# First-layer blocks of 512 columns as halves of 256, a changed order of each chunk's first blocks, and shorter zero matmuls

## The chip, the cores and the metric

The kernel runs on one core of one Trainium2 chip, in one launch. The metric is the device time of an execution in microseconds (us), the median over runs. Three runs of the kernel before took 183.96 to 184.36 us, median 184.15.

The core has a matrix engine (TensorE, PE in the profile; PEld are its weight loads), a vector engine (VectorE, DVE), an engine for functions of single elements (ScalarE, ACT), a general one (GpSimd, POOL), and a sequencer that mostly issues transfers (SyncE, SP). 16 DMA engines move data. TensorE writes into PSUM, an accumulator memory; the others read it from there. Engines run their own instruction streams and wait for each other through semaphores.

## What is computed

A recurrent linear attention over 768 time steps (batch 4, 8 heads, head size 48), and then a two-layer network with a SiLU over the 3072 resulting rows of 384 values:

```python
for t in range(S):
    kt, vt, rt = (k[:, :, t], v[:, :, t], r[:, :, t])
    cur = np.einsum('bhd,bhe->bhde', u[None] * kt, vt)
    y[:, :, t] = np.einsum('bhd,bhde->bhe', rt, state + cur)
    state = w[None, :, :, None] * state + np.einsum('bhd,bhe->bhde', kt, vt)
x = y.transpose(0, 2, 1, 3).reshape(B * S, H * D)
h = x @ w_in                                # 384 -> 2048
out = (h * (1.0 / (1.0 + np.exp(-h)))) @ w_out   # 2048 -> 384
```

All inputs and the output are float32; the kernel does most matmuls in 16 bits.

## The kernel before

*Chunks and units.* Time is cut into six chunks of 128 steps. A unit is one chunk of one batch element, so there are 24 units, numbered chunk by chunk: units 0 to 3 are chunk 0, and so on. Within a unit the recurrence is made parallel: r and k are scaled by powers of w, the part inside the chunk (for later units inside each half of it) is a masked product of r and k, and the part of earlier steps comes through a carried state.

*The attention part of an iteration.* The main loop (L748) takes units in pairs, i and i + 1, so that a chunk has two iterations: `b` is 0 for units 0 and 1 of the chunk, and 2 for units 2 and 3. On TensorE an iteration is: `sums` (L478: products of k and v, 32 matmuls of 48 columns with both halves, 16 in the last chunk), `product_halves` (L455: r times k, 32 products in float32, seen in the trace as 64 matmuls), some fillers (below), `outputs_halves` (L552 and L561, 32 matmuls each: the carried state's part and the part inside the chunk), and `turn` (L272: transposes of the next pair's r, and of k where that isn't done by transfers). VectorE masks the product (L462), forms the state (L495, L509) and adds a bonus term to the outputs (L401, `evict_halves`). `turn_y_dma` (L584) then has a DMA transpose write y into the tile `xT` of the chunk, 4 units x 3 parts x 128 columns, which the first layer reads. Later units' k goes through another DMA transpose (L321).

*The network part.* The first layer is cut into 16 blocks of 128 of the 2048 inner values. `l1(sc, 0, B, f)` for chunk `sc` and block `f` does three matmuls (L606, one for each 128 of the 384 inputs) over all four units of the chunk at once, 512 columns, into a PSUM tile `hps`, then ACT's SiLU (L615) into `gT`. In chunks 0 and 1 some blocks are done for two units at a time: 256 columns, two blocks to a PSUM tile. The second layer, `l2` (L628), is done unit by unit: four parts of four matmuls with 384 columns, then a copy (L634) and a store (L638). The very last unit's is split (L653).

*Fillers.* These pieces are put into a list and taken from it at fixed places of the loop by `fill(n)`: after `product_halves`, after the turn, and later in the iteration, so that TensorE has work while other engines prepare the next step of the attention. A chunk gives 16 fillers of the first layer (`first(sc)` for chunks 2 to 5) and 16 of the second (`second(sc)`). They are appended at L790, after the second pair's `turn_y_dma`; what is still in the list from the chunk before goes first. A filler of the first layer is one block. After the loop `fill` empties the list (L822).

*The beginning.* For units 0 to 5 the order of all work is written out by hand in the string `order` (L717); a word like `2*spin` calls `spin(2)`. `spin` (L178) multiplies zeros (the tile `idle`) into a PSUM tile that nobody reads; the order has six such matmuls right after `clear` near the start, and nine more, in groups of one or two, between the real work up to unit 7. `lk8`, `lr8` and the like are loads of a unit's k or r into one of eight buffers, issued on SP.

*PSUM.* `hps`, `ops`, `sp`, `yp`, `yT`, `zs` and `bc` share four buffers (tag "moe"), given out in turn; a new tile waits for the readers of the one that had its buffer. The product and the turn use two tiles of their own (`att`).

The whole order is fixed at build time (`manual_schedule`), so each engine runs its instructions exactly as written.

Of the kernel before, what the change touches and what calls it, by code (L numbers as in the profile page):

```python
# [8 lines left out]
FP = mybir.dt.float32  # L9
# [7 lines left out]
def kernel(  # L17
# [11 lines left out]
    nc = tc.nc  # L29

    B, H, S, D = r.shape
    C = 128
# [6 lines left out]
    NFT = DFF // 128  # L39
    NQ = HD // 128  # L40
# [7 lines left out]
    ps = ctx.enter_context(tc.tile_pool(name="ps", bufs=1, space=bass.MemoryType.PSUM))  # L48
    ctx.enter_context(tc.manual_schedule())

    def unit(i):
        return divmod(i, B)
# [15 lines left out]
    win = [big.tile([128, NQ, 512], F16, name=f"win{g}") for g in range(4)]  # L68
# [36 lines left out]
    idle = cst.tile([128, 512], F16)  # L105
# [69 lines left out]
            nc.scalar.copy(out=dst[i][:, :, D:64],  # L175
                           in_=idle[:, 0:128].rearrange("p (h d) -> p h d", h=H))

    def spin(n):  # L178
        zs = ps.tile([128, 512], FP, name="zs", tag="moe", bufs=4)
        for _ in range(n):  # L180
            nc.tensor.matmul(zs, idle[:, 0:128], idle, start=True, stop=True)

    def clear():
        for t in att:
# [18 lines left out]
    def spread_row(name, src):  # L203
        spread[name] = ps.tile([128, HD], FP, name="bc", tag="moe", bufs=4)
        nc.tensor.matmul(spread[name], ones, src, start=True, stop=True)
# [369 lines left out]
    xts = {}  # L575
# [23 lines left out]
    hpss = {}  # L599

    def l1_mm(sc, b0, nb, ft):
        m = B // nb
        hps = hpss[b0, ft] = ps.tile([128, m, nb * C], FP, name="hps", tag="moe", bufs=4)
        for f in range(m):
            for q in range(NQ):
                nc.tensor.matmul(hps[:, f, :].rearrange("p (b t) -> p b t", b=nb), win[(ft + f) // 4].rearrange("p q (t c) -> p q t c", c=4)  # L606
                                 [:, q, :, (ft + f) % 4],
                                 xts[sc][:, b0:b0 + nb, q, :],
                                 start=(q == 0), stop=(q == NQ - 1))

    def l1_silu(sc, b0, nb, ft):
        if sc not in gts:
            gts[sc] = wrk.tile([128, NFT, B * C], F16, name="gT", bufs=2)
        m = B // nb
        nc.scalar.activation(out=gts[sc][:, ft:ft + m, b0 * C:(b0 + nb) * C], in_=hpss[b0, ft],  # L615
                             func=AF.Silu)

    def l1(sc, b0, nb, ft):
        l1_mm(sc, b0, nb, ft)
        l1_silu(sc, b0, nb, ft)  # L620
# [56 lines left out]
        return [lambda ft=ft: l1(sc, 2, 2, ft) for ft in range(0, NFT, 2)]  # L677

    def first(sc):
        return [lambda f=f: l1(sc, 0, B, f) for f in range(NFT)]  # L680

# [2 lines left out]
    halved = [lambda ft=ft: l1(1, 0, 2, ft) for ft in range(0, NFT, 2)]  # L686

    def piece(word, f):
        b0, ft = word.split(".")
        f(0, *blocks[b0], int(ft))  # L690
# [6 lines left out]
        "wy": lambda: columns(nc.scalar, wpT, w, 0), "lnw": powers_r, "eK": exponents_k,  # L697
        "lamK": powers_k, "uc": copy_u, "wb": lambda: spread_row("w", w_row),
        "ub": lambda: spread_row("u", u_row), "lnwb": ln_w, "lamC": powers_c, "lamH": powers_h, "lamN": powers_n,
        "tab": silu_table, "clear": clear, "spin": lambda: None, "H": lambda: halved.pop(0)(),  # L700
    }
    unit_steps = {
        "T": turn, "rT": lambda i: decay_one(i, 0), "kT": lambda i: decay_one(i, 1),
# [12 lines left out]
    }  # L716
    order = """  # L717
        ur kz0 id itr lr0 wy pd0 ak0 cz2 kz3 itc wr mk wx cz1 mh lnw eK cg3 lamK kz4 kz1 lk1
        id16 lr1 pd3 lr3 lk3 clear 6*spin lv0 cg0 lv1 kz7 lr2 ak2 ku0 lv3 lr5 kz2 lv2 ub pd1 lv4
        lr4 lk4 lv5 pd2 lk5 lk7 lr6 lk6 uc T0 1*spin T1 lr7 lv7 kT0 pa4 rT0 ru0 ku1  # L720
        v160 pd5 lv6 rT1 kz6 rd0 kT1 wb ru1 P0 n0 2*spin rd1 P1 vu0 lnwb T2 n1 v161 2*spin
        pd7 lamC lamH lamN pa6 i_q0 V0 v162 tab rT2 e0 kT2 ku2 T3 1*spin yT0 V1 kz5 vu1 i_q1 ru2
# [9 lines left out]
    for word in order.split():  # L732
        if "*" in word:
            n, word = word.split("*")
            spin(int(n))
        if word in steps:
            steps[word]()
        elif word[0] == "L":
            piece(word[1:], l1_mm)
        elif word[0] == "G":  # L740
            piece(word[1:], l1_silu)
        else:
            unit_steps[word[:-1]](int(word[-1]))
# [4 lines left out]
    for i in range(B + 2, NU, 2):  # L748
        sc, b = unit(i)
# [39 lines left out]
        if b:  # L789
            fillers.extend((first(sc) if sc > 1 else rest_first(sc)) + second(sc))  # L790
# [62 lines left out]
```

## Time and profile before

| | us |
|---|---|
| median of three runs | 184.15 |
| the profiled execution | 185.49 |
| its span, first to last instruction | 183.8 |
| busy: TensorE matmuls | 174.5 |
| busy: TensorE weight loads (overlap the matmuls) | 113.9 |
| busy: GpSimd | 129.3 |
| busy: VectorE | 117.0 |
| busy: ScalarE | 115.8 |

One execution was recorded by the hardware profiler. A group row names the line, the engine, the operation, what is written from what, its form and count, and then the busy time, the mean duration in ns, and the idle time of the engine just before with what ended it. A row of the chain of waits has the start, the length and the piece of work, followed back from the last instruction; "issue" is time for which the profile knows no cause. A row of the timeline has start, length, engine, line, operation and count, where equal neighbours are merged. A row of the windows has a stretch, its length, TensorE's busy time and instruction count in it, the granted clock, the mean busy share of the DMA engines, and GB/s. The length of a merged row reaches to the end of its last instruction, and a matmul's end overlaps the next one's start: the duration of a matmul of 512 columns is 380 ns in the mean, while the next starts 216 ns after it. The TensorE clock was granted in full over the whole span.

### The profile page before, as it was taken

What the parts mean: (1) busy time and instruction counts of PE and PEld (TensorE: products, weight loads), DVE (VectorE), ACT (ScalarE), POOL (GpSimd) and SP (SyncE); (2) the same over time, 40 slices, a digit from 0 to 9 for tenths busy, and PEclk for the clock granted to TensorE, in tenths of its full rate; (3) what the DMA queues carried; (4) which work ended last, traced back from release to release, by engine and by line L of the source; (5) the groups of instructions that cost most, each with busy time, mean ns of one, the idle gap of its engine ahead of it and who ended that gap; (6) DMA issues with size and microseconds to landing.
All of it is one profiled execution on the core that took longest, in us unless ns stands there. A gap on an engine that the chain in (4) does not pass through costs nothing.

```text
span 183.8 us, 6611 instructions
## 1 busy us (share of the span) xinstructions
PE 174.5 (95%) x2801; PEld 113.9 (62%) x2801; DVE 117.0 (64%) x231; ACT 115.8 (63%) x208; POOL 129.3 (70%) x179
## 2 busy tenths in 40 slices
PE   7977899999899999999899999999999999999993
PEld 2555786588666976656556555657656566555562
DVE  5999728897977985865775955776944974000120
ACT  4471787699145797398597488797588781299200
POOL 7999999898899979869979769879769700000000
PEclk9999999999999999999999999999999999999999
DMA  5999999899697799999599999499799201410022
GB/s 95 238 192 216 178 175 200 154 224 225 129 189 210 114 202 184 199 183 202 114 178 177 162 209 213 92 183 160 183 197 250 49 4 46 128 43 0 10 79 86
DMA packets 102865, 27.89 MB, mean 152 GB/s; under 512 B 97586, under 2 KB 102324, under 8 KB 102836
## 3 DMA queue, kind: packets, MB, share of 16 engines
q1 hardware_dynamic: 98224, 23.86, 66.5%
q0 software_dynamic: 2176, 3.15, 10.1%
q10 hardware_dynamic: 2436, 0.46, 1.3%
q8 instruction: 22, 0.36, 0.8%
q14 instruction: 7, 0.06, 0.1%
HBM read 20.45 MB, written 4.72 MB: 137 GB/s over the span
## 4 chain that ended last, share of the span: by engine, by line
PE 72%; POOL 17%; DMA 5%; issue 5%; ACT 0%; POOLq 0%
PE ops L628 33%; PE hps L606 26%; DMA kin<-in_k_dram 5%; PE att L455 4%; POOL ku L240 4%; POOL rku_f L245 3%; PE att L272 3%; POOL vu L258 2%; POOL kc L248 2%; PE yp L552 2%; PE sp L478 2%; PE ops L653 1%; PE yp L561 1%; POOL win L84 1%; POOL wout L89 1%
## 5 line engine op out<-in xcount | busy, mean ns | idle before, releaser
L606 PE MATMUL hps<-xT,win 128*128 128x512 f16 (+1 forms) x360 | 66.3, 338 | 0.1
L615 ACT ACTIVATE gT<-hps 128x512 f16<-128x512 f32 x96 | 55.3, 597 | 12.2 <-PE hps L606 8.9
L628 PE MATMUL ops<-wout,gT 128*128 128x384 f16 x368 | 62.9, 326 | 0.1
L606 PEld LDWEIGHTS <-win 128*128 128x128 f16 x360 | 39.0, 114 | 21.1 <-issue 0.4
L628 PEld LDWEIGHTS <-gT 128*128 128x128 f16 x368 | 35.0, 98 | 23.9 <-ACT gT L615 0.8
L401 DVE TENSOR_TENSOR y<-yp,vu 64x384 f16<-64x384 f32 (+1 forms) x34 | 18.9, 555 | 11.3 <-PE yp L561 5.5
L245 POOL TENSOR_TENSOR rku_f<-ku,u_bc 128x384 f32<-128x384 f32 x24 | 24.2, 1010 | 1.4
L240 POOL TENSOR_TENSOR ku<-kin,rin 128x384 f32<-128x384 f32 x24 | 24.2, 1007 | 0.7 <-DMA rin<-in_r_dram 0.6
L258 POOL TENSOR_TENSOR vu<-vin,rku 128x384 f32<-128x384 f32 x24 | 19.6, 828 | 6.8 <-DVE rku L253 6.8
L289 DVE TENSOR_TENSOR rT<-att,lamR 112x512 f16<-112x512 f32 (+1 forms) x26 | 17.8, 684 | 4.2 <-PE att L272 3.8
L326 ACT COPY kT<-blocks 112x1024 uint16<-112x1024 uint16 x14 | 15.6, 1160 | 7.6 <-DMA blocks<-planes 7.5
L634 ACT COPY osb<-ops 128x384 f32<-128x384 f32 x20 | 9.4, 475 | 16.5 <-PE ops L628 12.5
L495 DVE TENSOR_TENSOR s<-sp,sdec 112x384 f32<-112x384 f32 x10 | 5.6, 557 | 16.0 <-PE sp L478 15.4
L636 DVE COPY osb<-ops 128x384 f32<-128x384 f32 x3 | 1.7, 557 | 21.3 <-PE ops L628 21.3
L462 DVE TENSOR_TENSOR am<-att,maskH 128x1024 f16<-128x1024 f32 x10 | 12.2, 1224 | 3.5 <-PE att L455 3.5
L343 DVE TENSOR_TENSOR rX<-att,lamR 48x256 f16<-48x256 f32 x32 | 13.5, 421 | 0.5
L263 ACT CAST v<-vin 128x384 f16<-128x384 f32 x16 | 7.9, 510 | 8.4 <-DMA vin<-in_v_dram 8.3
L253 DVE TENSOR_REDUCE rku<-rku_f 128x8 f32<-128x384 f32 x24 | 12.4, 542 | 0.9 <-POOL rku_f L245 0.9
L314 POOL TENSOR_TENSOR lnw_bc<-kin,lamN 128x384 f32<-128x384 f32 x7 | 7.0, 1001 | 8.0 <-DMA kin<-in_k_dram 6.4
L434 ACT CAST s1h<-s 48x384 f16<-48x384 f32 x16 | 8.2, 510 | 6.7 <-DVE s L495 6.6
L455 PE MATMUL att<-rT,kT 48*64 48x64 f32 x640 | 11.9, 220 | 0.2 <-issue 0.2
L455 PEld LDWEIGHTS att<-rT,kT 48*64 48x64 f32 x640 | 10.6, 135 | 0.3 <-issue 0.3
(106 smaller groups left out, 214.0 us busy)
## 6 DMA issues: line engine op xcount, KB each, us to landing
rin<-in_r_dram SPq DMA_DIRECT2D x24, 192.0 KB, 4.0
vin<-in_v_dram SPq DMA_DIRECT2D x24, 192.0 KB, 4.6
out_dram<-osb SPq DMA_DIRECT2D x23, 192.0 KB, 3.2
kin<-in_k_dram SPq DMA_DIRECT2D x22, 192.0 KB, 3.5
win<-in_moe_w_in_dram POOLq DMA_DIRECT2D x4, 384.0 KB, 6.3
wout<-in_moe_w_out_dram POOLq DMA_DIRECT2D x4, 384.0 KB, 6.6
kin<-in_k_dram ACTq DMA_DIRECT2D x2, 192.0 KB, 3.7
xT<-y SPq DMA_TRANSPOSE x9, 2.8
```

Of the source, the lines that this page charges most:

```text
L240: eng.tensor_tensor(out=L(i)["ku"], in0=kin[i % NIN][:, :, 0:D], in1=rin[i % NIN][:, :, 0:D], op=ALU.mult)
L245: eng.tensor_tensor(out=L(i)["rku_f"], in0=L(i)["ku"], in1=u_bc, op=ALU.mult)
L253: nc.vector.tensor_reduce(out=L(i)["rku"], in_=L(i)["rku_f"], axis=mybir.AxisListType.X, op=ALU.add)
L258: eng.tensor_tensor(out=L(i)["vu"], in0=vin[i % NIN], in1=L(i)["rku"].unsqueeze(2).broadcast_to([128, H, D]), op=ALU.mult)
L289: nc.vector.tensor_tensor(out=L(i)[key].rearrange("p g (y t) -> p y g t", y=2), in0=L(i)["t"][0:PR, :, x], in1=lam, op=ALU.mult)
L326: nc.scalar.copy(out=L(i)["kT"].rearrange("p g t -> p (g t)").bitcast(U16) .rearrange("p (n y) -> p n y", y=2), in_=turned[0:PR, i % 2].re ...
L343: nc.vector.tensor_tensor(out=rx[here], in0=L(i)["t"][there, x, 0], in1=(lamM if by_planes(i) else lamR)[there, :, 0:HC], op=ALU.mult)
L401: nc.vector.tensor_tensor(out=y16[a], in0=y[b, 0:HD], in1=vu[a], op=ALU.add)
L455: nc.tensor.matmul(a[o0:o0 + HC, j, e, p, :], kT[r0:r0 + D, p, HC * x:HC * x + HC], rT[r0:r0 + D, p, HC * x:HC * x + HC], start=True, stop ...
L606: nc.tensor.matmul(hps[:, f, :].rearrange("p (b t) -> p b t", b=nb), win[(ft + f) // 4].rearrange("p q (t c) -> p q t c", c=4) [:, q, :, ( ...
L615: nc.scalar.activation(out=gts[sc][:, ft:ft + m, b0 * C:(b0 + nb) * C], in_=hpss[b0, ft], func=AF.Silu)
L628: nc.tensor.matmul(opss[b], gts[sc][:, ft, b * C:(b + 1) * C], wout[:, ft, :], start=(ft == 0), stop=(ft == NFT - 1))
```

## The change

Three edits, all in what TensorE is given:

- `first(sc)` no longer makes a filler of one whole block. A new function `l1_half` does a block for two units, 256 columns: three matmuls into the left or right half of the block's PSUM tile, and the SiLU over all 512 columns after the right half. A filler is now two halves.
- The order of a chunk's first two fillers: the first does units 0 and 1 of blocks 0 and 1, the second does units 2 and 3 of both. Every later filler does both halves of one block. In chunk 2 the last six blocks stay whole.
- `spin` takes a number of columns, 100 by default, and does five matmuls for each that it did before; the six at the start keep 512 columns (the word `long`).

```diff
-    def spin(n):
+    def spin(n, cols=100):
         zs = ps.tile([128, 512], FP, name="zs", tag="moe", bufs=4)
-        for _ in range(n):
-            nc.tensor.matmul(zs, idle[:, 0:128], idle, start=True, stop=True)
+        for _ in range(n * (512 // cols)):
+            nc.tensor.matmul(zs[:, 0:cols], idle[:, 0:128], idle[:, 0:cols], start=True, stop=True)
...
+    def l1_half(sc, b0, ft):
+        if b0 == 0:
+            hpss[0, ft] = ps.tile([128, 1, B * C], FP, name="hps", tag="moe", bufs=4)
+        for q in range(NQ):
+            nc.tensor.matmul(hpss[0, ft][:, 0, b0 * C:(b0 + 2) * C].rearrange("p (b t) -> p b t", b=2),
+                             win[ft // 4].rearrange("p q (t c) -> p q t c", c=4)[:, q, :, ft % 4],
+                             xts[sc][:, b0:b0 + 2, q, :],
+                             start=(q == 0), stop=(q == NQ - 1))
+        if b0:
+            l1_silu(sc, 0, B, ft)
...
     def first(sc):
-        return [lambda f=f: l1(sc, 0, B, f) for f in range(NFT)]
+        whole = 6 if sc == 2 else 0
+        halves = [(b0, f) for b0 in (0, 2) for f in range(2)]
+        halves += [(b0, f) for f in range(2, NFT - whole) for b0 in (0, 2)]
+        return [lambda n=n: [l1_half(sc, *h) for h in halves[n:n + 2]]
+                for n in range(0, len(halves), 2)] + [
+                    lambda f=f: l1(sc, 0, B, f) for f in range(NFT - whole, NFT)]
...
-        id16 lr1 pd3 lr3 lk3 clear 6*spin lv0 cg0 lv1 kz7 lr2 ak2 ku0 lv3 lr5 kz2 lv2 ub pd1 lv4
+        id16 lr1 pd3 lr3 lk3 clear 6*long lv0 cg0 lv1 kz7 lr2 ak2 ku0 lv3 lr5 kz2 lv2 ub pd1 lv4
...
-            spin(int(n))
+            spin(int(n), *((512,) if word == "long" else ()))
```

In the built programs TensorE has 3011 matmuls instead of 2801, each with a weight load. The instructions of the other four engines, their transfers included, stand in the same order as before.

More of the change, by code (lines that the diff above doesn't have):

```diff
@@ L699 @@
         "ub": lambda: spread_row("u", u_row), "lnwb": ln_w, "lamC": powers_c, "lamH": powers_h, "lamN": powers_n,
-        "tab": silu_table, "clear": clear, "spin": lambda: None, "H": lambda: halved.pop(0)(),
+        "tab": silu_table, "clear": clear, "spin": lambda: None, "long": lambda: None, "H": lambda: halved.pop(0)(),
     }
```

## The prediction

> **What bounds the kernel now.** I read the busy shares first, then who TensorE (PE) waited for, then the chain of work that ended last, and last the trace around two odd gaps.
>
> ```profile
> span 183.8 us, 6611 instructions
> ...
> PE 174.5 (95%) x2801; PEld 113.9 (62%) x2801; DVE 117.0 (64%) x231; ACT 115.8 (63%) x208; POOL 129.3 (70%) x179
> ...
> q8 instruction: 22, 0.36, 0.8%
> ```
>
> PE is busy 95%, the others 62 to 70%. The third line is the queue that brings instructions: 22 packets. PE has 2801 matmuls and 2801 weight loads; 5602/22 is 255, so a packet is one block of 256 PE instructions (16.4 KB), fetched while the program runs.
>
> PE's waits from 20 us on:
>
> ```profile
> PE att L272 <- DMA kin<-in_k_dram: 1.0, 2, 0.6
> PE yp L561 <- issue: 0.5, 1, 0.5
> PE att L272 <- issue: 0.4, 1, 0.4
> ...
> PE att L455 <- issue: 0.2, 1, 0.2
> ```
>
> Three are put down to "issue": nothing the profile can name. The chain shows where:
>
> ```profile
> 38.46 9.68 DMA kin<-in_k_dram
> ...
> 48.19 0.44 PE att L272 x8
> ...
> 73.20 0.37 PE yp L552 x32
> ...
> 74.44 5.31 PE ops L628 x32
> ...
> 87.05 0.37 PE yp L552 x32
> 87.42 0.12 PE yp L561 x13
> 87.54 0.51 issue
> 88.05 0.34 PE yp L561 x19
> ...
> 88.98 4.66 PE hps L606 x21
> ...
> 100.50 0.37 PE yp L552 x32
> ...
> 101.51 0.43 issue
> 101.94 0.44 PE att L272 x9
> 102.38 5.31 PE ops L628 x32
> ...
> 180.83 0.27 ACT osb L660
> ```
>
> Until 48.19 the end is set by POOL and then by a load of k that lands at 48.14; PE stood idle for it. From 48.19 to 180.8 the chain is PE work piece after piece, broken only by the two "issue" gaps. So what is saved or added on PE behind 48.19 counts in full, and what changes ahead of it is first swallowed by the wait for k.
>
> The gaps cut a run of equal matmuls in two (13 and 19 of L561's 32; seven transposes of L272, then nine), so no operand was late. An undisturbed stretch from the first L552 to the end of the turn takes 74.44 - 73.20 = 1.24 us. The two with gaps take 88.98 - 87.05 = 1.93 and 102.38 - 100.50 = 1.88. So 0.69 + 0.64 = **1.33 us** are lost.
>
> Busy time from the start to chosen moments, for the count of matmuls behind "x":
>
> ```profile
> 0.00:83.13 83.13, 77.79 (x1369) 1.00 0.97 184
> 0.00:88.05 88.05, 82.20 (x1497) 1.00 0.98 183
> 0.00:97.58 97.58, 91.70 (x1625) 1.00 0.96 181
> 0.00:101.94 101.94, 95.63 (x1752) 1.00 0.97 180
> ```
>
> From one gap's end to the other's are 255 matmuls. With weight loads and the few instructions that only wait, the kernel's instruction order puts the first late ones at 3010 and 3522: exactly two blocks apart. The short gap in L455 (the 0.2 above) is at 962, eight blocks ahead of 3010. I conclude that **PE starves at block borders**. A border is crossed each 256 instructions, and most cost nothing. These were reached too fast: the block ahead was entered at 83.13 and 97.58 (128 and 127 matmuls earlier), 4.92 and 4.36 us before work resumed. The fetches, each seen as one packet in a tenth of a microsecond, began only at 85.8 and 98.5:
>
> ```profile
> q8 instruction: 1, 0.02, 54.9%
> ...
> q8 instruction: 1, 0.02, 121.8%
> ```
>
> Bursts of small matmuls (sums, product, outputs, turn) eat a block quickly; L606 and L628 eat it slowly. The sequencer also works ahead: the earliest fetch began when PE was 303 instructions short of its block. So I measure a border's lead from PE being 303 short to PE arriving. By positions and starts in the trace the gaps' leads are 5.1 and 4.7 us, stall included; every other border behind 48 us had 5.9 or more and lost nothing. The early one at 962 had 6.4, in a stretch where fetches start later.
>
> The Trainium skill ("Runtime: NRT & Kernel Launch", section "Instruction fetch mechanics") has the same 256-instruction blocks, but says that crossing a border is one queue bump, "mostly hidden". The rows disagree at these two borders.
>
> **The change part by part.** *Halves: price on PE.* A block of `first` is three matmuls of 512 columns and becomes six of 256. Split are ten blocks in chunk 2 and 16 each in chunks 3 to 5: 58 blocks, 174 matmuls more. Both widths run already, in dense stretches:
>
> ```profile
> 61.77 4.78 PE L606 MATMUL hps<-xT,win 128*128 128x256 f16 x42
> 66.38 0.81 PE L628 MATMUL ops<-wout,gT 128*128 128x384 f16 x4
> ...
> 62.01 4.31 PE L606 MATMUL hps<-xT,win 128*128 128x256 f16 x38
> ...
> 160.04 9.66 PE L606 MATMUL hps<-xT,win 128*128 128x512 f16 x44
> ...
> L606 PE MATMUL hps<-xT,win 128*128 128x512 f16 x216 | 49.2, 380 | 0.0
> L606 PE MATMUL hps<-xT,win 128*128 128x256 f16 x144 | 17.1, 273 | 0.1
> ```
>
> Less the last one's duration, (4.31 - 0.273)/37 = 109.1 ns and (9.66 - 0.380)/43 = 215.8 ns from start to start. Two halves take 2.4 ns more than a whole: 174 x 2.4 = **+0.42 us**, all on the path. Bounds: 0, and 0.65 (with the lead-in from 61.77 to 66.38, 4.61 us over 42 are 109.8 ns). The weight load doubles with the matmul and is in the 109 ns.
>
> *Halves: place on the instruction grid.* This is the large term. In the built order PE has 416 instructions more, so every border falls elsewhere. A chunk's two iterations become 1025 instructions, four blocks and one, so from chunk 3 on the borders return to nearly the same four places, until chunk 5 has shorter sums. Behind 48 us they lie in L628 and split L606 work, except five in outputs (the 7th, 1st, 6th and 16th of L552's 32, the 10th of L561's 32) and one in chunk 5's sums. Their leads, with the durations of before put in the new order, are 6.7 us and more: the shortest, chunk 5's L561, has ahead of it 0.3 us of halves, 2.0 of L628, 0.3 of sums, 1.0 of product, 2.7 of L628, 0.5 of outputs. Before, 5.9 was enough and 5.1 not. So both stalls go: **-1.33 us**. Bounds: 0 if they aren't tied to the grid, -1.33 if they are; I take the latter.
>
> *Units 0, 1 first.* The first `fill` item of a chunk needs only the transpose of the chunk's first two units; the second pair's is due one filler (6 x 109 = 0.65 us) later. Chunk 3 shows why this matters once the stall at 101.5 is gone:
>
> ```profile
> 103.00 1.22 SPq L584 DMA_TRANSPOSE xT<-y  x1
> ...
> DMA to landing us min/median/max: 2.7/2.8/4.0
> ...
> 107.53 1.67 PE L606 MATMUL hps<-xT,win 128*128 128x512 f16 x7
> ```
>
> This is the slowest of the nine; it lands at 107.0, 0.5 us ahead of its first reader. The stall sat behind the outputs that feed it, so without the stall PE arrives 0.64 earlier: 0.1 late with whole blocks, 0.5 in time with halves. I cost it at zero; without the halves' order it would be +0.1. In exchange, two accumulators stay open through one filler and ACT gets the first two SiLUs together, the first 0.3 us later. Both end within the same `fill`, no other tile is taken between them, and the order on DVE, ACT, POOL and SP, their DMAs included, is unchanged: zero.
>
> *Short zero matmuls.* Nine of 512 columns become 45 of 100. Their price is bounded by the nearest narrower row:
>
> ```profile
> 179.79 1.00 PE L653 MATMUL ops<-wout,gT 128*128 128x128 f16 x15
> ...
> L653 PE MATMUL ops<-wout,gT 128*128 128x128 f16 x16 | 1.1, 219 | 0.0
> ```
>
> (1.00 - 0.219)/14 = 55.8 ns for 128 columns, so 45 cost at most 2.51 us; by columns (100/512 of 215.8, 42 ns) 1.90. The nine cost 1.94 now. That is -0.04 to +0.57, and I take +0.05 since 100 is near 128. None of it reaches the end: all nine stand ahead of 48.19, where these waits follow:
>
> ```profile
> 17.14 0.33 PE L380 MATMUL att<-rT,kT 48*64 48x128 f32 x4 [1.02 <-DVE rT L289]
> ...
> 48.19 0.32 PE L272 MATMUL att<-ident,kin 64*112 64x64 f32 x4 [0.56 <-DMA kin<-in_k_dram]
> ```
>
> Three of the nine come behind 17.14: at most 15 x 55.8 - 3 x 215.8 = 0.19 us, less than 0.56. With that cover gone the price would be this 0.19. The lost time at 962 (two borders near 40 us have leads of 6.5) moves inside the same cover: zero; if the load of k moved with it, up to -0.4.
>
> The Trainium skill ("TensorE: Matmul & The Clock Gate", section "Back-to-back issue gap") gives some 81 ns a matmul for a stream of load and matmul pairs of 128 columns. By that estimate the 45 take 3.6 us, 1.7 more than now, and the part behind 17.14 takes 0.57, just the cover; the trace's 55.8 ns decides.
>
> **Sum.** On the profiled execution: 183.8 - 1.33 + 0.42 = 182.9 us of span. That run took 185.49 in all, 1.69 around its span; the unprofiled median is 184.15, 1.34 below it. I take the difference to the median: 184.15 - 0.91 = **183.24 us**.
>
> **Rivals.** *One border stalls again.* A transpose or load burst delays a fetch beyond the lead that I counted; the trace has fetches that began over 2.5 us after their block ahead was entered (85.8 against 83.13). One stall back: 184.15 - 0.66 + 0.42 = 183.91. Against it: the new leads exceed the need by 1.6 us.
>
> *Slower: the stalls are not there to be won.* The profiled run is 1.34 us longer than the median, nearly the 1.33 of the stalls: if it is the recording that delays the fetches, an unprofiled run hides the borders and only the halves' price remains: 184.15 + 0.42 = 184.57, up to 184.80 by the bound. It decides where an unrecorded fetch is over 0.7 us quicker. For it: the equality. Against it: 1.34 must also hold what recording costs at start and end, and the fetches stand behind the kernel's own transfers (the DMA share in the count rows is 0.96 to 0.98). By the Trainium skill's rule quoted above ("Runtime: NRT & Kernel Launch", "Instruction fetch mechanics") this would be the outcome.
>
> *More is won.* The load of k also moves with the early part: 183.24 - 0.39 = 182.85. Against it: the chain hangs that load on POOL, whose order is unchanged.
>
> *The chunk start waits.* Stalls gone, but PE then runs into a late transpose in each of four chunks. With 0.5 us of margin, a transpose 0.7 late costs 0.2 each: 184.04. The nine landings (2.7 to 4.0 us) speak against it.
>
> **How the numbers follow.** Forecast 0.58; one stall back 0.12; slower 0.19; more 0.06; chunk starts 0.05. The forecast's own range is 182.9 to 183.6 (halves at 0 to 0.65, with a few tenths of stall left). To leave no more than 2 in 10 out the range goes from 182.75 to 184.5, short of the slower case's centre. A measurement can tell 0.2% from no change, 0.37 us here: faster is below 183.78, slower above 184.52. Faster: forecast, more, and a third of one stall, 0.68. Slower: most of its case, 0.15. The rest, 0.17, is same.
>
> **What would show it.** Right: no "issue" wait of PE behind 48 us in a run of equal matmuls, the stretch from L552 to the turn's end at 1.24 us everywhere, halves at 109 ns, 23 or 24 packets on the instruction queue, the first L606 of a chunk without a wait, the k load still landing near 48. Wrong: a gap at another border, halves above 110 ns, a wait for xT, or stalls gone in the profile while the median stays.

## The result, and the profile after

| | before | after |
|---|---|---|
| median of 21 runs each, us | 184.15 | 184.73 |
| all runs, us | 182.75 to 185.18 | 183.75 to 186.29 |
| ratio after/before | | 1.0042, 95% [1.0021, 1.0062] |
| the recorded execution, us | 185.49 | 184.85 |
| its span | 183.8 | 183.1 |

The kernel became 0.39 to 1.14 us slower (the interval on 184.15), while the recorded execution of after is 0.64 us shorter than that of before. Both are true, and the study is about how they go together. (Single executions that a disturbance had lengthened are left out of the ratios, not of the medians.)

The profile page of after, the rows that answer to those of before:

```profile
span 183.1 us, 7027 instructions
...
PE 175.5 (96%) x3011; PEld 134.5 (73%) x3011; DVE 117.1 (64%) x231; ACT 115.6 (63%) x208; POOL 129.5 (71%) x179
...
q8 instruction: 23, 0.38, 0.9%
```

PE is busy 1.0 us more, and one more block of instructions is fetched. The granted clock of TensorE was full in the recording of before; in this one it is at half for 3.41 us from 14.42 us on (0.991 in the mean of the span), and the short zeros that fall into it start some 81 ns apart instead of 44. In this kernel L615 is `l1_half`'s matmul, L626 the SiLU, L639 the second layer and L645 its copy. PE's waits from 20 us on:

```profile
PE att L455 <- issue: 0.6, 1, 0.6
PE hps L615 <- DMA xT<-y: 0.2, 1, 0.2
```

The first is an early block border. Behind 48 us no "issue" is left; a wait for chunk 2's `xT` is new. The chain of waits of after (start, length, piece):

```profile
75.05 0.55 DVE y L401
75.60 0.03 issue
75.63 0.76 DVE rT L289 x2
76.39 4.06 DMA xT<-y
80.45 0.04 issue
80.50 2.78 PE hps L615 x24
...
87.38 0.37 PE yp L552 x32
87.74 0.28 PE yp L561 x32
88.03 0.59 PE att L272 x16
88.62 0.78 PE hps L615 x6
...
100.14 0.37 PE yp L552 x32
100.51 0.28 PE yp L561 x32
100.80 0.59 PE att L272 x16
101.39 5.31 PE ops L639 x32
...
159.22 10.48 PE hps L615 x96
...
180.18 0.27 ACT osb L671
```

Both places that had a gap in before now take 88.62 - 87.38 = 101.39 - 100.14 = 1.24 to 1.25 us, the undisturbed length. Chunk 5's 96 halves take 10.48 us; the same row of before's chain is

```profile
159.99 10.36 PE hps L606 x48
```

so sixteen split blocks cost 0.12 us, 58 of them 0.44. And up to 80.50 the end is now set by a chain of loads, POOL and DVE that leads to the transposes of y, instead of by PE.

Why these landed at 80.45, when in before they landed at 78.95 (75.706 + 3.248), can be read from two queues. SP's instructions, before and then after (start, length; the transposes are L584):

```profile
74.93 0.36 SPq L638 DMA_DIRECT2D out_dram<-osb  x1
75.71 1.70 SPq L584 DMA_TRANSPOSE xT<-y  x1
```

```profile
75.93 0.36 SPq L649 DMA_DIRECT2D out_dram<-osb  x1
76.39 1.24 SPq L584 DMA_TRANSPOSE xT<-y  x1
```

ACT's at the same place, before and then after:

```profile
74.01 0.51 ACT L263 CAST v<-vin 128x384 f16<-128x384 f32 x1 [0.71 <-DMA vin<-in_v_dram]
74.43 0.47 ACT L634 COPY osb<-ops 128x384 f32<-128x384 f32 x1
```

```profile
75.01 0.51 ACT L263 CAST v<-vin 128x384 f16<-128x384 f32 x1 [1.80 <-DMA vin<-in_v_dram]
75.43 0.47 ACT L645 COPY osb<-ops 128x384 f32<-128x384 f32 x1
```

A load of v lands 1.0 us later, so ACT's cast and the copy behind it are 1.0 later, so the store of that copy goes out 1.0 later, and the transposes stand behind the store on SP: 0.68 later, though their y is ready at 75.60 here and at 75.68 in before. (The chain names rT as the releaser, which the transposes don't read; SP was at the store's issue until 76.29.) The rest, 4.06 - 3.25 = 0.81 us, is the transposes' own duration. A fetch of instructions runs during both. In before it starts with them, 0.03 us behind their issue; in after it is found in a window of a tenth of a microsecond at 77.8, that is 1.44 us behind their issue, and is 0.88 long:

```profile
q8 instruction: 1, 0.02, 54.9%
```

### The profile page after: what moved, and what is told of

It is laid out like the page before. It is cut to its first block, busy times and chain, and to the rows that moved or that the text cites. A ratio compares the mean times of both kernels' runs of the same rounds, so it can differ in the third digit from the quotient of the medians.

```text
span 183.1 us, 7027 instructions
## 1 busy us (share of the span) xinstructions
PE 175.5 (96%) x3011; PEld 134.5 (73%) x3011; DVE 117.1 (64%) x231; ACT 115.6 (63%) x208; POOL 129.5 (71%) x179
## 4 chain that ended last, share of the span: by engine, by line
PE 56%; POOL 23%; DMA 9%; issue 5%; DVE 3%; SPq 2%; ACT 0%; POOLq 0%
PE ops L639 22%; PE hps L615 21%; POOL ku L240 5%; DMA rin<-in_r_dram 4%; POOL kc L248 4%; POOL rku_f L245 4%; PE att L455 3%; POOL vu L258 3%; PE att L272 2%; DMA kin<-in_k_dram 2%; DMA xT<-y 2%; PE hps L606 2%; SPq L73 2%; POOL sdec L516 1%; PE ops L664 1%
## 5 line engine op out<-in xcount | busy, mean ns | idle before, releaser
L639 PE MATMUL ops<-wout,gT 128*128 128x384 f16 x368 | 62.9, 326 | 0.0
L626 ACT ACTIVATE gT<-hps 128x512 f16<-128x512 f32 x96 | 55.1, 597 | 12.2 <-PE hps L615 5.0
L639 PEld LDWEIGHTS <-gT 128*128 128x128 f16 x368 | 35.0, 98 | 23.2 <-ACT gT L626 0.8
L615 PE MATMUL hps<-xT,win 128*128 128x256 f16 x348 | 40.0, 273 | 0.2 <-DMA xT<-y 0.2
L615 PEld LDWEIGHTS <-win 128*128 128x128 f16 x348 | 37.6, 113 | 1.2 <-issue 0.3
L606 PE MATMUL hps<-xT,win 128*128 128x256 f16 (+1 forms) x186 | 27.1, 298 | 0.0
L606 PEld LDWEIGHTS <-win 128*128 128x128 f16 x186 | 19.7, 114 | 4.0 <-issue 0.2
L645 ACT COPY osb<-ops 128x384 f32<-128x384 f32 x20 | 9.3, 477 | 16.0 <-PE ops L639 11.8
```

The lines of the kernel that those rows point to most:

```text
L615: nc.tensor.matmul(hpss[0, ft][:, 0, b0 * C:(b0 + 2) * C].rearrange("p (b t) -> p b t", b=2), win[ft // 4].rearrange("p q (t c) -> p q t c ...
L639: nc.tensor.matmul(opss[b], gts[sc][:, ft, b * C:(b + 1) * C], wout[:, ft, :], start=(ft == 0), stop=(ft == NFT - 1))
```

## The experiments

Each run was compared with the kernel before on the same chip; all compute the full result. The kernels differ in three things: how many blocks are halves, how long the later zero matmuls are, and by how many PE instructions the stream is moved. The last is set by splitting the six zero matmuls at the start into more, narrower ones of about the same total width. (The matmul behind them starts at 4.9 to 5.6 us in the kernels with split zeros, at 4.91 and 5.53 us in the two recordings of before.) The ratios are against before in the same batch; its medians differ by batch, from 184.10 to 184.38. Some expectations call theories by letters. C: the short zero matmuls do harm themselves. D: a fetch that falls into the transposes of y delays them, and a chunk's first block waits. E: borders with a short lead stall.

**Before once more, and each part alone.** First the kernel before, unchanged, for a second recording:

> The kernel before, unchanged, profiled once more and timed against itself. Its profile on record took 185.49 us, 1.34 over its median, and lost 1.33 us in two "issue" gaps of PE behind 48 us. Theory A (the gaps belong to every execution): two gaps again, at instructions 3010 and 3522, 0.6 to 0.7 us each. Theory B (the recorded execution was a slow one; in most, the fetches come in time): no gap or one behind 48 us, and a profiled time near 184.2. Ratio 1.000 within 0.002 either way.

Median 184.14, recorded 184.89, ratio 1.0017 [0.9989, 1.0044] for an unchanged kernel. PE waits only once behind 60 us, and not for instructions; its chain:

```profile
86.92 0.37 PE yp L552 x32
87.29 0.28 PE yp L561 x32
87.57 0.59 PE att L272 x16
88.16 4.66 PE hps L606 x21
...
99.68 0.37 PE yp L552 x32
...
100.99 5.31 PE ops L628 x32
...
128.84 4.59 DMA xT<-y
133.43 0.05 issue
133.48 3.43 PE hps L606 x15
```

From 86.92 to 88.16 are 1.24 us where the first recording took 1.93, with the same instructions at the same border, and from 99.68 to 100.99 1.31 us where it took 1.88. So the two stalls of 1.33 us in the recording of before are no fixed part of the kernel. In their place this execution has 0.6 us of wait for the transposes of chunk 4, which landed after 4.59 us.

The zero matmuls alone, which moves the stream by 72 instructions:

```diff
-    def spin(n):
+    def spin(n, cols=100):
...
-        for _ in range(n):
-            nc.tensor.matmul(zs, idle[:, 0:128], idle, start=True, stop=True)
+        for _ in range(n * (512 // cols)):
+            nc.tensor.matmul(zs[:, 0:cols], idle[:, 0:128], idle[:, 0:cols], start=True, stop=True)
```

> Only the nine zero matmuls become 45 of 100 columns; first-layer blocks whole as before. It moves the borders of 256 instructions by 72. Leads, counted as in the prediction with the stalls taken out: three short ones behind 48 us (5.3, 4.4 and 4.6 us, in the outputs of iterations near 99, 113 and 127 us) where the kernel before has two (4.4 and 4.1). Theory A: gaps there, some 1.5 us in all, and a time near that of before, 184.2 to 184.8. Theory B: hardly a gap, and 184.15 within 0.2. Theory C (the short zero matmuls themselves harm, by a lower granted clock or later starts in the first 20 us): slower by 0.3 us or more with a clock below 1.000 between 10 and 20 us, and PE later than before at the 48 us mark.

185.50, ratio 1.0072 [1.0037, 1.0107]: the part that I had costed at nothing is the dearest. The recorded execution (187.28, its longest) waits 1.7 us for chunk 2's `xT`. Then the halves alone, zeros long, stream not moved at the start:

```diff
-        return [lambda f=f: l1(sc, 0, B, f) for f in range(NFT)]
+        whole = 6 if sc == 2 else 0
...
+        return [lambda n=n: [l1_half(sc, *h) for h in halves[n:n + 2]]
```

> Only the halves, their order and the six whole blocks of chunk 2; zero matmuls of 512 columns as before. Without the 72 instructions of the zero matmuls the borders fall into the outputs of four iterations, with leads of 4.0, 4.4, 4.2 and 4.5 us. Theory A: four gaps near 99, 113, 126 and 140 us, 2.0 to 2.8 us in all, and 186.5 to 187.5. Theory B: few gaps, and the price of the halves alone, 184.15 + 0.42 = 184.57. Under theory C this one is free of the harm: 184.57 or less with a full clock.

184.96, 1.0048 [1.0019, 1.0077]; the 0.44 of the price lies in the interval. Then halves in the first two blocks of a chunk only:

```diff
-        whole = 6 if sc == 2 else 0
+        whole = NFT - 2
```

> Only each chunk's first two blocks as halves, units 0 and 1 first; the other 14 whole, zero matmuls of 512 columns. 24 matmuls more instead of 174: price 24 x 2.4 ns = 0.06 us. Three short leads (4.0, 5.1 and 4.5 us, near 99, 113 and 151 us). Theory A: two or three gaps, 1.0 to 1.6 us, 184.0 to 184.6. Theory B: 184.15 + 0.06 = 184.2.

184.13, 1.0016 [0.9988, 1.0044]: 24 more matmuls instead of 174, and nothing that can be measured.

**Is it the short zeros, or the 72 instructions?** One kernel keeps the long zeros and adds the 72 instructions at the start; another makes each later zero matmul one of 100 columns and adds none.

```diff
-            spin(int(n))
+            spin(int(n), *((73,) if word == "long" else ()))
```

> The kernel before, with the six zero matmuls at the start as 42 of 73 columns (the same columns in sum, while PE waits for the first loads anyway): it moves the borders of 256 instructions by the same 72 as the short zero matmuls did alone, and leaves the later zero matmuls at 512 columns. Short leads as there: 5.3, 4.4 and 4.6 us near 99, 113 and 127 us. If the grid made the short zeros alone slower (185.50 against 184.14): 185.0 to 185.8, and gaps at instruction 4034 or 4546. If the short zeros themselves did (theory C): 184.15 within 0.3.

```diff
-    def spin(n):
+    def spin(n, cols=100):
...
-            nc.tensor.matmul(zs, idle[:, 0:128], idle, start=True, stop=True)
+            nc.tensor.matmul(zs[:, 0:cols], idle[:, 0:128], idle[:, 0:cols], start=True, stop=True)
```

> Each of the nine later zero matmuls stays one matmul, of 100 columns instead of 512: the order and count of instructions are those of before, and PE has 9 x (216 - 44) = 1.5 us less to do in the first 38 us. Theory C (less work between the real matmuls lets the granted clock fall or the start slip): 184.4 or more, a clock of 0.5 for some microseconds between 10 and 25 us. If only the grid counts: 184.15 within 0.3.

185.50 (6 runs), 1.0088 [1.006, 1.0116], against 184.09, 1.0001 [0.9969, 1.0032]. Short zeros by themselves cost nothing that can be seen (theory C falls). A lower clock, its sign, doesn't go with them either: a stretch of 3.41 us at half clock stands in the first 23 us of the recordings of after, e3, e4 and e6, two with short zeros and two with long ones, and not in that of e2; over all executions the mean clock is below 0.995 in 16 of 100 with short zeros and in 28 of 152 of before. 72 instructions more, in a part of the program that is otherwise the same, cost 1.1 to 2.1 us. PE's waits behind 60 us in the run with 72 instructions, and then its chain:

```profile
PE hps L606 <- DMA xT<-y: 0.9, 1, 0.9
PE yp L561 <- issue: 0.4, 1, 0.4
```

```profile
76.20 4.17 DMA xT<-y
80.38 0.05 issue
80.42 3.43 PE hps L606 x15
```

The same two disturbances as in after, here with whole blocks: transposes issued late, at 76.20, with a fetch 1.21 us behind their issue and 4.17 to landing. A whole block needs all four units at once, and PE waits 0.9 us where after waited 0.2.

The changed kernel with long later zeros (the 72 instructions put at the start instead), and the changed kernel again:

> The changed kernel with its later zero matmuls at 512 columns again and the 72 instructions moved into the 42 short ones at the start: halves, and the changed kernel's own place of the borders, whose shortest lead behind 48 us is 6.7 us. If the halves' price of 0.42 is all: 184.55 within 0.3, like the changed kernel. If the short zeros cost something beside it: 0.2 to 0.5 less than the changed kernel in the same rounds. No gap behind 48 us in either case.

> The changed kernel once more, for a second profile and in the same rounds: 184.73 within 0.3 by the time on record. No gap of PE behind 48 us at a border, as in its first profile (the leads there are long); if one appears, a long lead does not protect. The first block of a chunk waits for xT by no more than 0.4 us.

185.14, 1.006 [1.0036, 1.0085] and 185.25 (7 runs), 1.0064 [1.003, 1.0099]. The cost doesn't depend on which zeros carry the 72 instructions. Both recordings wait for chunk 2's `xT` (0.4 and 0.2 us); neither has an "issue" behind 48 us.

**Other places on the grid.** Two blocks as halves with the short zeros (moved by 72), the same moved by 108, whole blocks moved by 108 and by 192 (all four with short zeros; 128 and 46 columns for the six at the start):

> Each chunk's first two blocks as halves, units 0 and 1 first, the other 14 whole, and the short zero matmuls: the grid of the runs at 185.50, with 24 matmuls more. Theory D (formed from the ten profiles so far): what the 72 instructions do is to bring a fetch of 16 KB 1.2 to 1.6 us behind the issue of chunk 2's transposes, which then land after 4.0 to 4.4 us instead of 2.7 to 3.5, and PE, due at 79.5, waits for xT. The order of the first two blocks gives 0.65 us of grace, so the wait falls from 1.05 us in the profile of the grid alone to 0.2 to 0.5: 184.7 to 185.0. Theory E (the loss is at PE's gaps at borders, with two short leads, 4.4 and 4.0 us near 113 and 127 us): no recovery, 185.3 to 185.7, two gaps.

184.89, 1.0028 [0.9995, 1.0062], in theory D's range and not in E's; the recorded execution (187.59, its longest) has 1.1 us of wait for chunk 2's `xT` and two border stalls.

> As the one before with 108 instead of 72 instructions in front (six zero matmuls at the start as 24 of 128 columns): one short lead instead of two (3.8 us near 126 us), and the fetch that met chunk 2's transposes some 36 instructions earlier, about 0.5 us. Theory D: the transposes of chunk 2 land 3.5 to 4.2 us after issue, wait 0 to 0.4; 184.2 to 184.8. Theory E: one gap of up to 0.9 us instead of two: 184.4 to 185.0, and below the one before.

184.68, 1.0032 [0.9999, 1.0066]; no wait of PE behind 60 us in the recording.

> The same 108 instructions in front with all blocks whole. Theory D: without the grace of the halves' order the wait for chunk 2's xT is 0.65 us longer than in the one before, at most 1.05: slower than it by 0.3 to 0.7 us, 184.7 to 185.3. Theory E: the same one gap and no other difference: equal to it within 0.2.

184.59, 1.0009 [0.9971, 1.0047]: the difference to the run before it, which theory D forecast, isn't seen. The recording has two pauses: 0.2 us until 79.94, just behind the landing of the transposes at 79.89, and 0.4 us until 81.64, which the profile puts down to ACT.

> All blocks whole and 192 instructions in front: four short leads behind 48 us (4.4, 3.8, 4.8 and 4.8 us near 61, 73, 88 and 140 us), while the fetch near chunk 2's transposes falls about 2 us ahead of their issue and so outside. Theory D: no wait for chunk 2's xT; a gap only where lead is under what the fetch takes there (start 2.8 + 0.9 + 1.5 us near 73): 0.5 to 1.5 us there, which comes ahead of the outputs that feed xT and so moves everything: 184.6 to 185.6. Theory E: four gaps, 2 us or more: 186 to 187.

185.55, 1.0094 [1.0065, 1.0123], as slow as the worst, and here the recording doesn't help: the transposes land in 2.75 us, one border stalls by 0.3, and the recorded execution (185.13) is the shortest of the twelve. What the others lose isn't known.

**Forecasting the collision.** From the distance of each border to the transposes I forecast at which shifts a fetch would fall into them, and took halves moved by 60 and 120, whole blocks moved by 48 and 84:

```diff
-            spin(int(n), *((73,) if word == "long" else ()))
+            spin(int(n), *((85,) if word == "long" else ()))
```

(85 columns for 60, 46 for 120, 102 for 48, 64 for 84.)

> The changed kernel with long later zero matmuls and 60 instructions at the start instead of 72 (six zero matmuls as 36 of 85 columns). No short lead behind 48 us (all 6.5 or more), and by the estimated fetch times no fetch within 0.1 to 2.7 us behind the issue of the transposes of chunks 2, 3 and 4. Theory D: chunk 2's transposes land after 2.7 to 3.5 us, no wait for xT over 0.2 us; 184.3 to 184.8, below the 185.14 of 72 instructions by 0.4 or more. Theory E: as with 72 instructions, 185.1 within 0.3.

185.62, 1.005 [1.0021, 1.0079]. PE's waits behind 60 us, and then two lines on the transposes:

```profile
PE hps L615 <- DMA xT<-y: 0.6, 1, 0.6
```

```profile
L584 SPq DMA_TRANSPOSE xT<-y x1: 1222/1222/1222, 77.3 to 77.3; - x1
...
DMA to landing us min/median/max: 4.3/4.3/4.3
```

The fetch came 1.91 us behind the issue, inside the transposes, where I had it outside.

> The same with 120 instructions. Leads behind 48 us 5.5 or more, as good as before, but fetches fall into the transposes of chunks 3 and 4, and half into those of chunk 2. Theory D: those of chunks 3 and 4 land after 3.5 to 4.5 us; with the grace of the halves' order PE waits 0 to 0.5 us at each; 185.0 to 185.8, above the one before by 0.4 or more. Theory E: equal to it within 0.3.

184.64, 1.0016 [0.9992, 1.004]; fetch at 0.31, landing 3.35 us after issue, no wait.

> The kernel before with 48 instructions at the start. The fetch near chunk 2's transposes comes some 0.8 us or more ahead of their issue. Two short leads (3.7 us near 99, 4.6 near 113). Theory D: no wait for xT near 80 us; one gap of up to 0.8 us near 99 at most; 184.1 to 184.7. Theory E: one or two gaps, 184.5 to 185.3.

184.27, 1.0003 [0.9977, 1.0029]; the fetch starts behind the landing, 2.74 us to landing, no wait for `xT`.

> The kernel before with 84 instructions at the start. The fetch falls fully into chunk 2's transposes. Two short leads (4.4 us near 113, 4.1 near 126). Theory D: they land after 3.9 to 4.5 us, PE waits 0.6 to 1.2 us near 80; 185.1 to 185.8, above the one before by 0.6 or more. Theory E: two gaps as in the one before and the same time within 0.3.

184.05, 0.9985 [0.9958, 1.0012]; fetch at 0.55, landing after 3.31 us. Its chain is PE all through chunk 2:

```profile
72.57 0.37 PE yp L552 x32
...
79.12 3.24 PE hps L606 x15
...
86.42 0.37 PE yp L552 x32
```

Three of these four came out on the other side of what was forecast (60, 120, 84). In each of them PE waits for chunk 2's transposes where these landed late and doesn't where they landed early; what failed was telling from the instruction count when a fetch starts. In g2 a fetch did meet chunk 3's (1.95 us behind, 4.64 to landing at 107.66), and the halves' order covered it: the second filler, which reads them, started at 107.70, 0.15 late.

So the times alone don't prove theory D: its ranges held in e9, e10, e12 (not for the reason given) and g3, and failed in e11, g1, g2 and g4; theory E's held in e10, e11 and g4. What speaks for D is in the traces.

**Between two neighbours.** Last, whole blocks moved by 60, between two places that cost nothing, and the changed kernel's halves with long zeros moved by 84 instead of 72:

> Whole blocks, late zero matmuls long, TensorE's stream moved by 60 instructions: between 48 (184.27) and 84 (184.05), and 12 short of 72 (185.50). Collision of a fetch with the transposes of chunk 2's xT: the fetch starts 1.5 to 2.3 us behind their issue, they land after 4.0 us or more, and the first reader near 81 waits 0.6 to 1.2 us; 185.0 to 185.8. A steady trend with the shift, or anything the number of instructions at the start costs by itself: 184.1 to 184.3, like both neighbours, with no such wait.

184.54, 1.0019 [0.9994, 1.0044]: missed again. The transposes were issued late (76.46), but the fetch started at 81.15, behind their landing, so they took 2.75 us and PE didn't wait.

> The changed kernel's halves with late zero matmuls long, moved by 84 instructions instead of its 72. Collision: the fetch starts 0 to 0.8 us behind the transposes' issue, they land within 3.6 us, no wait near 81; the price of the halves alone is left, 184.4 to 184.8. If the halves or the long start cost more by something else: 185.1 or more, as at 72 (185.14) and 60 (185.62).

184.18, 0.9993 [0.9963, 1.0024]. Twelve instructions more than in the run of halves with long zeros (1.006 [1.0036, 1.0085]) and the intervals don't touch. But one reason in the expectation is wrong. The lines on the transposes, and then the chain:

```profile
L584 SPq DMA_TRANSPOSE xT<-y x1: 1222/1222/1222, 75.5 to 75.5; - x1
...
DMA to landing us min/median/max: 4.2/4.2/4.2
```

```profile
72.78 0.37 PE yp L552 x32
...
79.33 3.27 PE hps L615 x30
...
86.70 0.37 PE yp L552 x32
```

A fetch did fall into them (1.16 us behind), and they took 4.2 us; they were only issued in time, at 75.53, and landed at 79.69, just ahead of the second filler at 79.33 + 0.65. It takes both, a late issue and a collision.

**All recordings side by side.** "Stretch" is from the first L552 near 73 us to the first near 87; "fetch" is its start behind the issue of chunk 2's transposes. All from the timelines of the recorded executions, and the instruction queue's packets.

| blocks | moved by | run | issue behind L552 | fetch | landing | stretch | median of runs | ratio |
|---|---|---|---|---|---|---|---|---|
| whole | 0 | before | 2.58 | 0.03 | 3.25 | 13.85 | 184.15 | - |
| whole | 0 | e1 | 2.58 | 0.25 | 3.45 | 13.90 | 184.14 | 1.0017 |
| whole | 0 | e6 | 3.45 | none | 2.96 | 14.09 | 184.09 | 1.0001 |
| whole | 48 | g3 | 2.58 | none | 2.74 | 13.85 | 184.27 | 1.0003 |
| whole | 60 | h1 | 3.28 | none | 2.75 | 13.85 | 184.54 | 1.0019 |
| whole | 72 | e5 | 3.28 | 1.21 | 4.18 | 14.92 | 185.50 | 1.0088 |
| whole | 84 | g4 | 2.58 | 0.55 | 3.31 | 13.85 | 184.05 | 0.9985 |
| whole | 108 | e11 | 2.71 | 0.94 | 3.97 | 14.53 | 184.59 | 1.0009 |
| whole | 192 | e12 | 2.87 | -0.79 | 2.75 | 14.17 | 185.55 | 1.0094 |
| two blocks halved | 0 | e4 | 2.58 | 0.34 | 3.52 | 13.97 | 184.13 | 1.0016 |
| two blocks halved | 72 | e9 | 3.88 | 1.49 | 4.47 | 15.16 | 184.89 | 1.0028 |
| two blocks halved | 108 | e10 | 2.58 | 0.32 | 3.50 | 13.87 | 184.68 | 1.0032 |
| halves | 0 | e3 | 2.58 | 0.35 | 3.54 | 14.11 | 184.96 | 1.0048 |
| halves | 60 | g1 | 3.52 | 1.91 | 4.27 | 14.64 | 185.62 | 1.0050 |
| halves | 72 | after | 3.34 | 1.44 | 4.06 | 14.26 | 184.73 | 1.0042 |
| halves | 72 | e8 | 3.48 | 1.45 | 3.99 | 14.32 | 185.25 | 1.0064 |
| halves | 72 | e7 | 3.72 | 1.40 | 4.01 | 14.59 | 185.14 | 1.0060 |
| halves | 84 | h2 | 2.81 | 1.16 | 4.16 | 13.92 | 184.18 | 0.9993 |
| halves | 120 | g2 | 2.62 | 0.31 | 3.35 | 13.92 | 184.64 | 1.0016 |

(e2, whose landing isn't in the trace, issued 4.45 behind and has 15.89.) Issue plus landing says what the stretch becomes: with whole blocks 6.4 and less leaves 13.85 to 14.09, 6.7 gives 14.53, 7.5 gives 14.92; halves stand 7.0 (h2) and lose from 7.4 on. Two stretches are lengthened by something else: e12's by a border stall of 0.3 us, and e3's by 0.2, spread over its thirty halves from 80.00 on (3.63 us against h2's 3.44) without a wait that the profile names. The medians follow this only loosely. Where the sum is 7.4 or more the ratios are 1.0042 to 1.0088, but for e9; yet e3 and e12 are as slow (1.0048 and 1.0094) with sums of 6.1 and 5.6. One recorded execution of a kernel doesn't tell what its median waits for, so the collision is shown in recordings and its share in the medians is argued.

## Why the prediction was wrong

**The step that failed is the -1.33.** "Before, 5.9 was enough and 5.1 not. So both stalls go: -1.33 us", and "I take the difference to the median". The stalls are real and at block borders (in the twenty recordings PE has 23 pauses over 0.15 us that the profile calls "issue", and all stand at the same place, to one instruction, in a block of 256), but they come and go between executions. Three recordings have before's own instruction order: before has two of about 0.6, e1 and e6 none, though e1 crossed the same two borders with leads of 4.4 and 4.1 us, which are before's without the stalls. In e3 and e4, where the halves move the later borders, the expectations had counted four and three short leads, and one border each stalls (0.5 and 0.3). So a border at the same place with the same lead stalls or doesn't, and a rule for leads drawn from one recording doesn't hold. The new order's own leads were counted rightly, the shortest behind 48 us is 6.7 in after too, and no border there stalls; but nothing was won by it. The median execution of before has nothing of them left to give: its span is 182.4 to 182.7 us in five batches of 23 to 35 executions, 1.1 to 1.4 below the recorded one's 183.8. That is the equality which the prediction saw (1.34 against 1.33) and gave 0.19. The rival "the stalls are not there to be won" was right in kind, 184.57 against 184.73. Whether recording causes them, as it said, is open: all five of these recordings are 0.66 to 1.34 us above their kernel's median, but of the fifteen with a moved stream some are above and some below, and what lies around the span is 1.7 to 1.8 us in recorded and other executions alike (2.0 in e12's recorded one). On the Trainium skill's sentence that crossing a border is "mostly hidden" ("Runtime: NRT & Kernel Launch", section "Instruction fetch mechanics") this trace agrees in the mean: most borders cost nothing, single ones 0.2 to 1.3 us.

**The halves' price was right.** Forecast +0.42, bounds 0 and 0.65. The two chain rows give 0.44. Over the whole program: from the first L552 behind 59 us to the start of the last matmul, less all pauses (what two neighbours' starts lie over 0.1 us further apart than such neighbours do in the median), ten recordings with whole blocks have a median of 118.41 us, seven with halves 118.81, so 0.40.

**"DVE, ACT, POOL and SP, their DMAs included, is unchanged: zero" was wrong.** The order is unchanged, the times are not: chunk 2's transposes landed 1.50 us later. 0.68 came through SP's queue, which passes a late load of v on to the transposes behind ACT's copy and a store; 0.81 came with the fetch. The prediction had noticed that the new grid moves the fetches, and looked only at what PE waits for, not at what the fetches run into. The row was on the table: the slowest of "2.7/2.8/4.0" us, at 103.00, is the one with a fetch 0.91 us behind it. (These are the six of the nine transposes whose landing the trace has; the prediction read them as nine landings.) The rival "the chunk start waits", given 0.05, was of the right kind, though in one chunk and not in four.

**"Units 0, 1 first" was right, and in the recordings worth more than was thought.** It was costed at zero, as cover of 0.65 us against a late `xT`. It was drawn on at once: of the 0.9 us that whole blocks wait at the same shift, after waits 0.2.

**Short zero matmuls: right for the columns (e6: 1.0001), wrong for the count.** Whatever they cost was to be hidden by the load of k that ended at 48.14. But PE waits for the load in only five of the twenty recordings, so the cover isn't always there. In after it isn't: the border in L455 that moved to 43.55 stalls,

```profile
43.55 0.35 PE L455 MATMUL att<-rT,kT 48*64 48x64 f32 x9 [0.64 <-issue]
```

and no wait for k follows. What before loses there instead (0.2 at instruction 962, 0.6 for k) makes up for it: the L552 near 60 us starts at 60.41 in after and 60.52 in before. Moved by 84, no border stalls there and k is in time, and that L552 starts at 59.54 (g4) and 59.63 (h2). In the recordings that is how h2, with all its halves, comes out level with before. The half clock in after's recording costs little by then: the second recording of the same kernel (e8) has none and starts the same L552 at 60.29.

**The sum as measured:** +0.44 for the halves, some +0.2 for chunk 2's transposes, nothing from the stalls: 184.15 + 0.6 = 184.8, against 184.73. That it fits to 0.1 is partly luck: the 0.2 is from one recorded execution, and beside another batch of before the same kernel cost 0.6 to 1.8 us (e8).

What stays open: why 192 instructions cost 1.4 us; when a fetch starts (it was forecast wrongly for 60, 84 and 120, and again for h1 and h2); what delays the load of v in some recordings; why the halves alone (e3) cost as much as with the 72 instructions, though their transposes weren't late; and what single unrecorded executions, which spread over 2 us, wait for. The clock explains little of that spread: of before's executions that the ratios use, the 17 with a mean clock below 0.995 have a median of 184.28 us, the other 118 of 184.09. No version is faster than before with certainty (g4: 0.9985 [0.9958, 1.0012]).

## What to carry to other kernels

Before a stall in a profile is booked as a gain, hold the recorded execution's time and span against the median: a stall as long as the difference between the two may not be in the median at all, as here, and a second recording of the unchanged kernel costs one run and shows whether it stays. Adding or removing instructions on a streamed engine moves its instruction fetches along the time of all other transfers, so a part that is free by its work can cost 1 us by its count; test it by adding as many idle instructions and nothing else. Where a consumer has half a microsecond of margin on a transfer, an order that lets it start on half of the data is cheap insurance.

## What the hardware showed

- *A fetch lengthens transposes that it falls into.* The trace has a landing for 114 DMA transposes of y in twenty recordings. 39 with no fetch between issue and landing took 2.72 to 2.96 us. Where the fetch had started ahead of their issue, 25 took 2.73 to 3.53; where it started up to 0.9 us behind it, 24 took 3.01 to 3.86. Of 26 with a start 0.9 us or more behind, 22 took 3.97 to 4.71 and four 2.74 to 2.75 (starts 2.32 or more behind). The fetch itself is one packet of 16 KB that takes 0.88 to 1.95 us.
- *The time goes into single packets.* The transposes move packets of 256 bytes. In 38 of the 39 without a fetch none of these takes over 0.07 us; in 17 of the 22 that took 3.97 and more the longest takes 1.2 to 2.1 us (1.52 in after, 1.66 in e5), longer than the fetch that it meets.
- *A block is not usable when it lands.* Where PE stalled at a border it went on 1.2 to 1.6 us after the packet had landed, and no border was crossed sooner than 1.2 us after.
- *Narrow matmuls.* From start to start in dense runs: 216 ns at 512 columns, 109 at 256, 44 at 100 (the short zeros).
